# Chunk 0's units 0 and 1: the score maximum subtracted by TensorE, and the calls of one engine listed anew

## The chip, the cores and the metric

The kernel runs on one core of a Trainium2 chip. The time is the device time of one execution in microseconds (us); a kernel's time is the median of its runs. The engines go by short names: PE is TensorE (PEld its weight loads), DVE is VectorE, ACT is ScalarE, POOL is GpSimd, SP is SyncE, which issues DMA transfers. Each engine works through its own instructions in the order in which they stand; between engines semaphores make one wait for another.

## The reference

Two stages. First an attention over blocks: q, k and v are 4 batches x 8 heads x 768 positions x 64, cut into 8 blocks of 96. A matrix of 8x8 for each head, `sort_net`, is normalised five times by rows and columns and mixes the blocks of k and v. Each block of q then attends to its mixed block alone. The result, 3072 tokens x 512, goes through a layer with a cosine gate.

```python
for _ in range(5):
    P = np.exp(P - np.max(P, axis=-1, keepdims=True))
    P = P / (np.sum(P, axis=-1, keepdims=True) + 1e-09)
    P = P / (np.sum(P, axis=-2, keepdims=True) + 1e-09)
k_sorted = np.einsum('bhij,bhjcd->bhicd', P, k_b)      # v_sorted likewise
scores = scale * np.matmul(q_b, k_sb.transpose(0, 1, 2, 4, 3))
scores = scores - np.max(scores, axis=-1, keepdims=True)
attn = np.exp(scores)
attn = attn / (np.sum(attn, axis=-1, keepdims=True) + 1e-09)
x = np.matmul(attn, v_sb)                  # then heads side by side: 3072 x 512
h = x @ w_in                               # 512 -> 2048
out = (h * np.cos(h)) @ w_out              # 2048 -> 512
```

## The kernel before

The 3072 tokens are cut into 8 chunks (`n`) of 384: four units (`u`) of 96 positions, all 8 heads. For a unit PE makes 8 score tiles of 96x96 in PSUM (`s_ps`, tile `sc`), DVE takes the maximum of each row and head (`s_max`, tile `mx`) and subtracts it into SBUF (`s_sub`, tile `s`), and ACT takes the exponential (`expo`, tile `p_buf`). PE turns the probabilities (`p_ps`, tile `pps`), an engine copies them to SBUF (`p_ev`, tile `p_turned`), PE weights the values with them (`av_products`, tile `av`; a column of ones beside the values gives the sums), DVE normalises (`av_norm`, tiles `r` and `xn`), PE turns the result (`x_ps`, tile `xps`), and an engine copies it into `xT` (`x_ev`).

Chunk 0 goes ahead as soon as the mixing matrix is there, so its keys are made by `kp` (48 products in three tiles `ks`) and copied by `k_place` in halves of four units, its values by `v0` in eight groups of 8 dimensions (tile `vs`) and copied by `v0e` into `vS`. `v_permute` on POOL brings the columns of dimensions 32 to 63 into order for groups 4 to 7. The mixing matrix is spread for these products by `block` on PE and `spread` on DVE (tiles `bl`, `bd`, `bdv`).

The layer is `h` = up product, cosine on ACT (tile `c`), gate on DVE (tile `gg`), down product (tile `o`). For chunk 0 the up product is done in halves of the tokens: `up_four(h, g, part)` for token half `h` (units 0 and 1, or 2 and 3) and group `g` of four of the 16 feature tiles, then `cos_four`, `gate_four`, and `down_four(ts, q)` for 128 tokens `ts` and feature group `q`; `down_out` copies and stores. For chunks 1 to 7 it is `up`, `down` and the lists given to `moe_up` and `moe_down`, into which scores, keys and values of later chunks are put.

The order of work is that of the calls in the program, written out by hand: tiles come from pools in the order of the calls, `B` is a pool of three PSUM buffers of two banks (`big`) and `C` one of two buffers of a bank (`acc`), and each engine's instructions stand as its calls come. A tile of a pool can be written once the last reader of the tile before it in its buffer is done. `fill=` and `keep_warm` add matmuls on zeros that nothing reads. The exponential and the cosine need different tables on ACT, which a table load changes. GpSimd's queue also issues most loads; from the first `v_permute` to the loads of chunk 2 its order is: the four pieces of `v_permute`, four loads of `w_out`, the ones beside the values (`ones(0)`), six copies of keys for chunk 1 (`kxp`), zeros in `q_turned`, the second halves of k and v, zeros and picks, q of chunk 2, and four more pieces of `v_permute`.

Units 2 and 3 of chunk 0 stay on the old path in both kernels, and so do all units of chunks 1 to 7.

## Time and profile before

| what | value |
|---|---|
| median of 3 runs | 231.24 us (231.17 to 231.74) |
| the profiled execution | 231.24 us, of which the span of its instructions is 229.5 us |
| PE, DVE, ACT, POOL busy | 221.8, 170.8, 154.3, 95.9 us |
| PE matmuls of the layer, up and down of chunks 1 to 7 | 78.4 and 76.2 us |
| read from HBM, written | 27.27 MB, 6.29 MB |

A row of the timeline has the start in us, the duration in us, the engine, the line in the kernel, the operation, the tile written and the tile read with partitions x elements, and how many such instructions are put together; in brackets stands the idle time of the engine before it and what ended it. A row of a group (by line and form) has, behind the first bar, the busy us of all and the mean ns of one. A row of the chain has start, duration, engine, tile and line: the chain leads back from the last instruction to what released it, or to the instruction before it on its engine.

### The profile page before, as it was taken

Reading aid. Unit: us, or ns where it says so; the run is one execution under the profiler, and the core shown is the slowest. Engines: PE = TensorE matmul, PEld = TensorE weight load, DVE = VectorE, ACT = ScalarE, POOL = GpSimd, SP = SyncE. Lnnn points to the kernel's source line nnn. Section 1 sums busy time; section 2 is a strip of 40 time slices with the busy share of each in tenths; the row PEclk is TensorE's granted clock in tenths of the full one; section 3 lists DMA queues with packets and bytes.
Section 4 is the critical chain, followed back from the end, with each engine's and each line's share of the span. In section 5 each row is a group of like instructions: output and inputs, shape, how many; then the busy total and the mean of one; then the engine's idle time right before and its main releaser. Section 6 shows DMA issues by size and latency. Waiting matters only on the chain.

```text
span 229.5 us, 5537 instructions
## 1 busy us (share of the span) xinstructions
PE 221.8 (97%) x2268; PEld 137.8 (60%) x2268; DVE 170.8 (74%) x295; ACT 154.3 (67%) x207; POOL 95.9 (42%) x121
## 2 busy tenths in 40 slices
PE   8789999999999999999999999999999999999994
PEld 3368898567765566655665456655665566555554
DVE  6769968978798778868589977987699769646700
ACT  5659877777889758797688466736674667716521
POOL 7999999399960197944509002700000000000000
PEclk9999999999999999999999999999999999999999
DMA  5999999995999799767979839953934440351012
GB/s 64 228 195 207 202 207 224 208 223 161 121 126 194 172 135 153 133 130 145 159 136 150 125 70 156 213 92 72 180 129 81 91 160 0 69 147 46 0 46 94
DMA packets 67833, 31.21 MB, mean 136 GB/s; under 512 B 56416, under 2 KB 63200, under 8 KB 67552
## 3 DMA queue, kind: packets, MB, share of 16 engines
q0 software_dynamic: 24048, 13.64, 43.6%
q1 hardware_dynamic: 43472, 17.02, 34.7%
q8 instruction: 18, 0.29, 0.5%
q10 hardware_dynamic: 288, 0.20, 0.3%
q14 instruction: 7, 0.06, 0.1%
HBM read 27.27 MB, written 6.29 MB: 146 GB/s over the span
## 4 chain that ended last, share of the span: by engine, by line
PE 85%; DVE 7%; ACT 3%; POOL 2%; issue 2%; ACTq 0%; DVEq 0%; POOLq 0%
PE h L684 32%; PE o L709 28%; PE h L873 5%; PE o L894 5%; PE av L640 3%; PE sc L453 3%; PE ks L420 2%; DVE s L840 2%; DVE mx L836 2%; PE o L1232 2%; ACT p_buf L583 1%; PE xps L671 1%; PE sc L518 1%; PE vs L464 1%; PE qps L276 1%
## 5 line engine op out<-in xcount | busy, mean ns | idle before, releaser
L684 PE MATMUL h<-xT,w_in_t 128*128 128x384 bf16 x448 | 78.4, 326 | 0.0
L709 PE MATMUL o<-w_out_t,gg 128*128 128x512 bf16 x320 | 76.2, 379 | 0.0
L688 ACT ACTIVATE c<-h,half_pi 128x768 f32<-128x768 f32 x56 | 50.5, 902 | 25.8 <-PE h L684 24.8
L692 DVE TENSOR_TENSOR gg<-c,h 128x768 bf16<-128x768 f32 x56 | 52.6, 948 | 19.4 <-ACT c L688 19.4
L684 PEld LDWEIGHTS <-w_in_t 128*128 128x128 bf16 x448 | 42.2, 98 | 26.3 <-DVE xT L267 0.6
L709 PEld LDWEIGHTS <-gg 128*128 128x128 bf16 x320 | 28.7, 98 | 28.4
L583 ACT ACTIVATE p_buf<-s 96x768 bf16<-96x768 f32 x32 | 26.6, 843 | 5.7 <-DVE s L505 4.0
L187 POOL COPY vperm<-kv 64x768 bf16<-64x768 bf16 (+2 forms) x12 | 28.4, 2406 | 4.0 <-DMA kv<-in_v_dram 4.0
L505 DVE TENSOR_TENSOR s<-sc,mx 96x384 f32<-96x384 f32 (+1 forms) x33 | 24.3, 735 | 1.6
L503 DVE TENSOR_REDUCE mx<-sc 96x4 f32<-96x384 f32 (+1 forms) x33 | 24.0, 727 | 0.2 <-PE sc L518 0.2
L653 DVE TENSOR_TENSOR xn<-av,r 96x512 bf16<-96x512 f32 x32 | 22.0, 686 | 1.1
L138 POOL DMA_DIRECT2D kv<-in_q_dram x24 | 16.0, 681 | 0.8 <-issue 0.8
L265 ACT COPY kv<-o 128x512 f32<-128x512 f32 (+2 forms) x10 | 5.2, 524 | 14.0 <-PE o L709 11.4
L265 ACT CAST kTs<-ks 128x512 bf16<-128x512 f32 (+1 forms) x18 | 11.0, 630 | 5.3 <-PE ks L420 4.4
L651 DVE RECIPROCAL r<-av 96x8 f32<-96x8 f32 x32 | 6.3, 198 | 9.4 <-PE av L640 9.0
L894 PE MATMUL o<-w_out_t,gg 128*128 128x512 bf16 x48 | 11.7, 379 | 0.0
L138 POOL DMA_DIRECT2D q_mem<-in_q_dram x16 | 10.7, 687 | 1.8 <-DMA kv<-in_v_dram 1.3
L267 DVE COPY kv<-o 128x512 f32<-128x512 f32 (+1 forms) x5 | 3.1, 612 | 11.1 <-PE o L1232 8.5
L873 PE MATMUL h<-xT,w_in_t 128*128 128x192 bf16 x128 | 11.1, 246 | 0.0
L453 PE MATMUL sc<-kTs,q_turned 128*128 128x96 bf16 x152 | 11.1, 206 | 0.0
L873 PEld LDWEIGHTS <-w_in_t 128*128 128x128 bf16 x128 | 10.5, 98 | 0.0
L611 POOL CAST held<-q_turned 96x1 f32<-96x1 bf16 x2 | 0.4, 182 | 23.8 <-DMA q_turned<-q_mem 16.2
(135 smaller groups left out, 283.4 us busy)
## 6 DMA issues: line engine op xcount, KB each, us to landing
out_dram<-kv SPq DMA_DIRECT2D x12, 256.0 KB, 2.7
out_dram<-o_s SPq DMA_DIRECT2D x10, 256.0 KB, 3.5
w_in_t<-in_moe_w_in_dram POOLq DMA_DIRECT2D x4, 512.0 KB, 11.6
w_out_t<-in_moe_w_out_dram POOLq DMA_DIRECT2D x4, 512.0 KB, 12.1
kv<-in_k_dram POOLq DMA_DIRECT2D x2, 768.0 KB, 9.9
kv<-in_v_dram POOLq DMA_DIRECT2D x2, 768.0 KB, 13.1
pair<-in_k_dram POOLq DMA_DIRECT2D x2, 768.0 KB, 12.3
kv<-in_v_dram POOLq DMA_DIRECT2D x6, 256.0 KB, 5.2
```

Source lines behind the costliest of these rows:

```text
L138: nc.gpsimd.dma_start(out=q_heads[:, i, :, e], in_=src[:, ih * IC + i, :, e])
L187: nc.gpsimd.tensor_copy(dst, src)
L503: nc.vector.reduce_max(mx[:], scv, axis=AX.X)
L505: nc.vector.tensor_tensor(s, scv, mx.to_broadcast(list(s.shape)), op=ALU.subtract)
L583: nc.scalar.activation(p[:, :, :blk], s_t.pop((n, u)).rearrange("p e h c -> p (e h) c"), AF.Exp, scale=scale)
L653: nc.vector.tensor_tensor(xn.rearrange("p h e d -> p e h d"), avv[:, :, :, :D], r.to_broadcast([blk, 2, H2, D]), op=ALU.mult)
L684: nc.tensor.matmul(h[:, f2, :w], w_in_t[:, kk, f * 128:(f + 1) * 128], xT[n][:, kk], start=(kk == 0), stop=(kk == KC - 1))
L688: nc.scalar.activation(c[:], h[:, :, :w], AF.Sin, bias=half_pi[:, 0:1])
L692: nc.vector.tensor_tensor(gt[n, fp // 2][:, f:f + 2], c[:], h[:, :, :w], op=ALU.mult)
L709: nc.tensor.matmul(o[:], gt[n, f // 4][:, f % 4, ts * 128:(ts + 1) * 128], w_out_t[:, f, :], start=(f == 0), stop=(f == FC - 1))
L873: nc.tensor.matmul(o[:, part, f2 * w:(f2 + 1) * w], w_in_t[:, kk, f * 128:(f + 1) * 128], xT[0][:, kk, h * w:(h + 1) * w], start=(kk == 0) ...
L894: nc.tensor.matmul(out_ps[ts][:], gt[0, q][:, f % 4, ts * 128:(ts + 1) * 128], w_out_t[:, f, :], start=(f == 0), stop=(f == FC - 1))
```

## The change

Units 0 and 1 of chunk 0 (`PULL`) lose `s_sub`. In its place DVE negates the maximum into two bf16 numbers, the rounded value and what the rounding left (`s_neg`, 96x8 each), and PE adds both to the scores in PSUM by products with the identity (`s_add`: two banks, two numbers, 384 columns each, accumulating). The exponential reads the scores from PSUM (`s_t` is None for these units). The score products of these units write 48 columns each and start the accumulation once a bank.

The ones beside chunk 0's values are written by ACT in the second softmax round, as the exponential of zeros, no longer by POOL.

The calls from the first key product on are listed anew, one engine's work to a call: `up`, `down`, `batch`, `k_sort_g`, `v_sort_b`, `moe_up`, `moe_down` and their like are replaced by calls for products, copies, cosine and gate apart (`uh`, `uc`, `ug`, `dn`, `dc`, `bt`, `kg`, `kge`, `vb`, `vbe` ...). The queues of GpSimd and SP keep their order, but for the ones. From the weighted values of chunk 1's unit 3 on, the order of each other engine's work is that of before too, but for the places where a call stood after five of eight matmuls of a `down` and now stands after four. What is ahead of it is another order. The diff, with the list up to that point:

```diff
@@ -366,6 +366,10 @@
             n = (D - 12 - VN) // 2 * blk
             t = vperm[64:, VN * blk + (it - 1) * n:VN * blk + it * n].bitcast(FP32)
             A.copy(t, nones[64:].to_broadcast([64, n // 2]))
+        if it == 1:
+            A.activation(
+                vS[0][:, :, D:D + 1], nones[:blk].unsqueeze(1).to_broadcast([blk, 4 * NB, 1]),
+                AF.Exp)
         normalize(it, (less if it < 4 else sorted_by)[:])
         if it < 2:
             nc.vector.memset(pick[:, nb - 1:, it * PB + PB - 1:(it + 1) * PB], 0.0)
@@ -576,13 +580,15 @@
         qk_part(n, u, [hp], pool or acc, tag)
 
     def expo(n, u, on_pe=False):
-        p = p_bufs[cnt[0] % NP]
+        p, s = p_bufs[cnt[0] % NP], s_t.pop((n, u))
         cnt[0] += 1
 
 
         nc.scalar.activation(
-            p[:, :, :blk], s_t.pop((n, u)).rearrange("p e h c -> p (e h) c"), AF.Exp,
-            scale=scale)
+            p[:, :, :blk] if s is not None else p[:, :, :blk].rearrange(
+                "p a (t x) -> p a t x", x=2),
+            s.rearrange("p e h c -> p (e h) c") if s is not None else s_view(n, u).rearrange(
+                "p a x t -> p a t x"), AF.Exp, scale=scale)
         if u == 0 and n in (NQ, NQ + 1):
 
             w = 2 * H2 * blk
@@ -632,8 +638,7 @@
             xT[n] = xtp.tile([128, KC, TC], BF16, name="xT", tag="xT")
         a = big.tile([128, 2, 512], FP32, name="av", tag="big")
         keep_warm(fill, a[:, 0], 256)
-        pT.pop((n, u))
-        pt = pT_wide.pop((n, u))
+        pt = pT_wide[n, u]
         for hp in range(2):
             for h2 in range(H2):
                 e = hp * H2 + h2
@@ -811,11 +816,12 @@
                 hp, c = a // H2, (u * H2 + a % H2) * blk
                 for x in range(2):
                     rows = slice(x * D, (x + 1) * D)
-                    m, w = a % H2 * nb + u, HT if a % H2 == H2 - 1 else 64
+                    m, w = a % H2 * nb + u, HT if u in PULL or a % H2 == H2 - 1 else 64
                     keys = kT[0][rows, 2 * hp].rearrange("p m t -> p (m t)")
                     nc.tensor.matmul(
                         o[:, x, a * HT:a * HT + w], q_of(0, hp)[rows, c:c + 128],
-                        keys[:, m * HT:m * HT + w], start=True, stop=True)
+                        keys[:, m * HT:m * HT + w], start=a == 0 or u not in PULL,
+                        stop=u not in PULL, skip_group_check=u in PULL)
             return
         if u < 2:
             by_half(n, u, o)
@@ -841,6 +847,27 @@
             s_t[n, u].rearrange("p e h (t x) -> p (e h) x t", x=2), s_view(n, u),
             ps.pop(("mx", n, u))[:].unsqueeze(2).to_broadcast([blk, 2 * H2, 2, HT]),
             op=ALU.subtract)
+
+    PULL = (0, 1, )
+
+    def s_neg(n, u):
+        mx = ps.pop(("mx", n, u))
+        t = sp.tile([blk, 2, H2, blk], FP32, name="s", tag="s")
+        less_m = ps["mn", n, u] = t[:, 0, 0, :2 * H2].bitcast(BF16).rearrange(
+            "p (z a) -> p z a", z=2)
+        nc.vector.tensor_scalar(less_m[:, 0], mx[:], -1.0, None, op0=ALU.mult)
+        nc.vector.scalar_tensor_tensor(
+            less_m[:, 1], mx[:], -1.0, less_m[:, 0], op0=ALU.mult, op1=ALU.subtract)
+
+    def s_add(n, u):
+        o, less_m = ps["s", n, u], ps.pop(("mn", n, u))
+        for x in range(2):
+            for z in range(2):
+                nc.tensor.matmul(
+                    o[:, x, :2 * H2 * HT], ident[:blk],
+                    less_m[:, z].unsqueeze(2).to_broadcast([blk, 2 * H2, HT]),
+                    start=False, stop=z == 1, skip_group_check=True)
+        s_t[n, u] = None
 
     def p_ps(n, u, pool, tag, fill=0):
         p = pb.pop((n, u))
@@ -904,190 +931,303 @@
         copy_on(eng, o_s[:], out_ps[ts][:])
         store(0, ts, o_s)
 
-    wz = iter(range(40, D, 4))
-    kz = iter(range(6, 12))
-
-    def k_next():
-        k_sort_g(next(kz) * 4, A, *C)
-
-    def w_next(eng=A, pool=None, tag="acc"):
-        v_sort_g(next(wz), 4, eng, pool or acc, tag)
-
...
+    def uh(n, fp):
+        h = ps["h", n, fp] = big.tile([128, 2, 512], FP32, name="h", tag="big")
+        for f2 in range(2):
+            f = fp * 2 + f2
+            for kk in range(KC):
+                nc.tensor.matmul(
+                    h[:, f2, :TC], w_in_t[:, kk, f * 128:(f + 1) * 128], xT[n][:, kk],
+                    start=(kk == 0), stop=(kk == KC - 1))
+
+    def uc(n, fp):
+        c = ps["c", n, fp] = cosp.tile([128, 2, TC], FP32, name="c", tag="c")
+        nc.scalar.activation(c[:], ps["h", n, fp][:, :, :TC], AF.Sin, bias=half_pi[:, 0:1])
+
+    def ug(n, fp):
+        if (n, fp // 2) not in gt:
+            gt[n, fp // 2] = gp.tile([128, 4, TC], BF16, name="gg", tag="gg")
+        f = fp % 2 * 2
+        nc.vector.tensor_tensor(
+            gt[n, fp // 2][:, f:f + 2], ps.pop(("c", n, fp))[:],
+            ps.pop(("h", n, fp))[:, :, :TC], op=ALU.mult)
...
+    blocks.append(block([pick[:, :, z * PB:(z + 1) * PB] for z in (1, 0)]))
+    kp(2, *B)
+    k_place(2, A, 1)
+    kp(0, *B)
+    values_matrix()
+    kp(1, *B)
+    k_place(0, A, 0)
+    k_place(2, A, 0)
+    v0(3, *C)
+    k_place(0, A, 1)
+    k_place(1, V, 0)
+    k_place(1, A, 1)
+    v_permute(slice(0, 64), 32, False, 8, 40)
+    v0e(3, A)
+    s_ps(0, 0)
+    s_max(0, 0)
+    s_neg(0, 0)
+    v_permute(slice(0, 64), 40, False, 8, 48)
+    v_permute(slice(0, 64), 48, False, 8, 56)
+    s_ps(0, 3)
+    v0(1, *C)
+    v0(0, *B)
+    v0e(1, A)
+    v0e(0, A)
+    s_add(0, 0)
+    expo(0, 0, True)
+    s_max(0, 3)
+    s_sub(0, 3)
+    expo(0, 3, True)
+    v_permute(slice(0, 64), 56, False, 8, 64)
+    s_ps(0, 1)
+    v0(6, *C)
+    s_max(0, 1)
+    v0(4, *C)
+    v0e(6, A)
+    s_neg(0, 1)
+    p_ps(0, 0, *B)
+    p_ev(0, 0, V)
+    s_ps(0, 2)
+    s_add(0, 1)
+    v0e(4, A)
+    v0(5, *C)
+    expo(0, 1, True)
+    s_max(0, 2)
+    v0(7, *C)
+    v0e(7, V)
+    v0e(5, A)
+    v0(2, *B)
+    p_ps(0, 1, *B)
+    p_ps(0, 3, *C, fill=1)
+    s_sub(0, 2)
+    v0e(2, A)
+    load_w_out(0)
+    p_ev(0, 1, V)
+    av_products(0, 0)
+    av_norm(0, 0, True)
+    expo(0, 2, True)
+    av_products(0, 1)
+    p_ps(0, 2, *C, fill=1)
+    p_ev(0, 3, A)
+    av_norm(0, 1, True)
+    av_products(0, 3, fill=3)
+    x_ps(0, 0, *C)
+    p_ev(0, 2, A)
+    av_products(0, 2, fill=2)
+    x_ev(0, 0, A)
+    x_ps(0, 1, *B)
+    av_norm(0, 3, True)
+    x_ps(0, 3, *C)
+    x_ev(0, 1, A)
+    q_products(1, 1, 0, 16, *B)
+    av_norm(0, 2, True)
+    x_ev(0, 3, A)
+    load_w_out(1)
+    q_place_half(1, 1, 0, V)
+    q_place_half(1, 1, 1, A)
+    q_products(1, 0, 0, 16, *C)
+    load_w_out(2)
+    load_w_out(3)
+    q_place_half(1, 0, 1, V)
+    q_place_half(1, 0, 0, V)
+    x_ps(0, 2, *C)
+    x_ev(0, 2, V)
+    up_four(0, 1, 0)
+    up_four(0, 1, 1)
+    cos_four(0, 1)
+    gate_four(0, 1)
+    up_four(0, 0, 0)
+    up_four(0, 0, 1)
+    up_four(1, 0, 0)
+    up_four(1, 0, 1)
+    cos_four(0, 0)
+    gate_four(0, 0)
+    cos_four(1, 0)
+    gate_four(1, 0)
+    kxp(2)
+    up_four(0, 3, 0)
+    up_four(0, 3, 1)
+    cos_four(0, 3)
+    gate_four(0, 3)
+    kxp(0)
+    up_four(0, 2, 0)
+    up_four(0, 2, 1)
+    kxp(1)
+    up_four(1, 2, 0)
+    cos_four(0, 2)
+    up_four(1, 2, 1)
+    cos_four(1, 2)
+    gate_four(0, 2)
+    up_four(1, 3, 0)
+    up_four(1, 3, 1)
+    z_turned(1)
+    down_four(0, 0)
+    load(kbuf, 0, kin_d[1])
+    s_ps(1, 0)
+    load(vbuf, 64, vin_d[1])
+    gate_four(1, 2)
+    cos_four(1, 3)
+    gate_four(1, 3)
+    picks(pick_pair, (2, 3))
+    s_ps(1, 1)
+    s_max(1, 0)
+    z_vperm()
+    last = block([pick_pair[:]], *C)
+    down_four(0, 1)
+    z_turned(0)
+    up_four(1, 1, 0)
+    spread(bds[1], last)
+    up_four(1, 1, 1)
+    cos_four(1, 1)
+    s_sub(1, 0)
+    p_pads()
+    s_max(1, 1)
+    s_sub(1, 1)
+    gate_four(1, 1)
+    ks(4, *C)
+    kse(4, A)
+    ks(5, *B)
+    kse(5, A)
+    down_four(0, 2)
+    down_four(0, 3)
+    s_ps(1, 3)
+    s_ps(1, 2)
+    down_four(1, 0)
+    expo(1, 0, True)
+    load_q(2)
+    down_four(1, 1)
+    expo(1, 1, True)
+    p_ps(1, 0, *B)
+    s_max(1, 3)
+    s_sub(1, 3)
+    expo(1, 3, True)
+    s_max(1, 2)
+    p_ps(1, 1, *B)
+    p_ev(1, 1, A)
+    load_pair(pair, kin_d, 0 * CD // 2, 1 * CD // 2)
+    p_ev(1, 0, V)
+    load_pair(pair, kin_d, 1 * CD // 2, 2 * CD // 2)
+    v_permute(slice(64, 128), 0, True, 16, 16)
+    down_four(1, 2)
+    av_products(1, 0)
+    v_permute(slice(64, 128), 16, True, 16, 32)
+    v_permute(slice(64, 128), 32, True, 16, 48)
+    s_sub(1, 2)
+    v_permute(slice(64, 128), 48, True, 16, 64)
+    av_products(1, 1)
+    av_norm(1, 1, True)
+    down_out(0, A)
+    av_norm(1, 0, True)
+    down_four(1, 3)
+    expo(1, 2, True)
+    p_ps(1, 3, *B)
+    x_ps(1, 1, *C)
+    p_ev(1, 3, V)
+    p_ps(1, 2, *B)
+    down_out(1, A)
+    down_four(2, 0)
+    x_ev(1, 1, A)
+    down_four(2, 1)
+    av_products(1, 3)
...
```

`uh`, `uc` and `ug` are the three parts of `up`; `dn` is four matmuls of `down`, and the others are cut from their old functions in the same way.

Three places of the order, before and now. First DVE, in chunk 0's softmax, from the first maximum to the copy of turned probabilities after the last subtraction. Names: `mx` maxima, `sc` a unit's scores, `s` the subtracted scores (or, now, the negated maximum), `p_turned` probabilities turned, `vS` values. Before:

```order
L836 TENSOR_REDUCE mx_420<-sc_391 96x8
L840 TENSOR_TENSOR s_432<-sc_391,mx_420 96x8x2x48
L836 TENSOR_REDUCE mx_461<-sc_434 96x8
L840 TENSOR_TENSOR s_513<-sc_434,mx_461 96x8x2x48
L836 TENSOR_REDUCE mx_525<-sc_465 96x8
L840 TENSOR_TENSOR s_539<-sc_465,mx_525 96x8x2x48
L836 TENSOR_REDUCE mx_554<-sc_496 96x8
L267 COPY p_turned0_136<-pps_542 96x768
L840 TENSOR_TENSOR s_580<-sc_496,mx_554 96x8x2x48
L267 COPY p_turned2_138<-pps_584 96x768
```

Now:

```order
L842 TENSOR_REDUCE mx_416<-sc_399 96x8
L858 TENSOR_SCALAR s_418<-mx_416 96x8
L859 SCALAR_TENSOR_TENSOR s_418<-mx_416,s_418 96x8
L842 TENSOR_REDUCE mx_465<-sc_423 96x8
L846 TENSOR_TENSOR s_467<-sc_423,mx_465 96x8x2x48
L842 TENSOR_REDUCE mx_497<-sc_471 96x8
L858 TENSOR_SCALAR s_509<-mx_497 96x8
L859 SCALAR_TENSOR_TENSOR s_509<-mx_497,s_509 96x8
L267 COPY p_turned0_136<-pps_512 96x768
L842 TENSOR_REDUCE mx_554<-sc_522 96x8
L267 CAST vS_106<-vs_556 96x64x8
L846 TENSOR_TENSOR s_595<-sc_522,mx_554 96x8x2x48
```

The units come in the order 0, 3, 1, 2 in both. Two subtractions of 96x768 are gone, two pairs on 96x8 are there, the first copy of turned probabilities stands one maximum earlier, and a copy of values stands ahead of the last subtraction.

Second ACT, from the copies of chunk 0's last turned probabilities to its first cosines (`c` from `h`); `xps` are turned results, `qps` the turned q of chunk 1. Before:

```order
L265 COPY p_turned1_137<-pps_594 96x768
L265 COPY p_turned3_139<-pps_635 96x768
L265 COPY xT_607<-xps_648 128x4x96
L265 COPY xT_607<-xps_678 128x4x96
L265 COPY q_turned1_92<-qps_693 64x2x4x96
L879 ACT_TABLE_LOAD
L879 ACTIVATE c_762<-h_721,half_pi_111 128x768
L879 ACTIVATE c_776<-h_741,half_pi_111 128x768
```

Now:

```order
L265 COPY p_turned1_137<-pps_585 96x768
L265 COPY p_turned3_139<-pps_624 96x768
L265 COPY xT_600<-xps_651 128x4x96
L265 COPY xT_600<-xps_669 128x4x96
L265 COPY xT_600<-xps_678 128x4x96
L265 COPY q_turned1_92<-qps_684 64x2x4x96
L906 ACT_TABLE_LOAD
L906 ACTIVATE c_753<-h_736,half_pi_111 128x768
L906 ACTIVATE c_791<-h_757,half_pi_111 128x768
```

One more copy into `xT` stands ahead of the table load, and the copy of q is of the other four heads; it waits for DVE's copy out of the same tile `qps`.

Third DVE, where chunk 1's scores start, around the spread of the second mixing matrix (`bd1`). Before:

```order
L405 TENSOR_TENSOR bd1_149<-maskp_147,bl_897 128x128
L836 TENSOR_REDUCE mx_947<-sc_926 96x8
L885 TENSOR_TENSOR gg_778<-c_936,h_907 128x4x192
L840 TENSOR_TENSOR s_970<-sc_926,mx_947 96x8x2x48
L836 TENSOR_REDUCE mx_977<-sc_938 96x8
L840 TENSOR_TENSOR s_998<-sc_938,mx_977 96x8x2x48
L836 TENSOR_REDUCE mx_1005<-sc_989 96x8
L836 TENSOR_REDUCE mx_1033<-sc_1017 96x8
L840 TENSOR_TENSOR s_1045<-sc_989,mx_1005 96x8x2x48
L840 TENSOR_TENSOR s_1056<-sc_1017,mx_1033 96x8x2x48
L651 RECIPROCAL r_1091<-av_1072 96x8
L653 TENSOR_TENSOR xn_1093<-av_1072,r_1091 96x2x4x64
```

Now:

```order
L912 TENSOR_TENSOR gg_819<-c_903,h_865 128x4x192
L842 TENSOR_REDUCE mx_922<-sc_892 96x8
L409 TENSOR_TENSOR bd1_149<-maskp_147,bl_925 128x128
L846 TENSOR_TENSOR s_962<-sc_892,mx_922 96x8x2x48
L842 TENSOR_REDUCE mx_967<-sc_913 96x8
L846 TENSOR_TENSOR s_969<-sc_913,mx_967 96x8x2x48
L912 TENSOR_TENSOR gg_755<-c_960,h_942 128x4x192
L842 TENSOR_REDUCE mx_1039<-sc_1000 96x8
L846 TENSOR_TENSOR s_1041<-sc_1000,mx_1039 96x8x2x48
L842 TENSOR_REDUCE mx_1044<-sc_1009 96x8
L267 COPY p_turned0_136<-pps_1030 96x768
L846 TENSOR_TENSOR s_1076<-sc_1009,mx_1044 96x8x2x48
```

The units now come as 0, 1, 3, 2, each subtraction right after its maximum but for the last, the gate of the group finished last stands behind two of them, and a copy of turned probabilities stands ahead of the last subtraction.

More of the change, by code (lines that the diff above doesn't have):

```diff
@@ new lines, in vbe, with dn @@
+    def vbe(b, d0, nd, eng):
+        copy_on(
+            eng, vS[0][:, b * 2 * NB:(b + 1) * 2 * NB, d0:d0 + nd],
+            ps.pop(("vb", b, d0))[:blk].rearrange("p t n -> p n t"))
+    def dn(n, ts, q):
+        if q == 0:
+            out_ps[n, ts] = acc.tile([128, Dm], FP32, name="o", tag="acc")
+        for f in range(q * 4, q * 4 + 4):
+            nc.tensor.matmul(
+                out_ps[n, ts][:], gt[n, q][:, f % 4, ts * 128:(ts + 1) * 128], w_out_t[:, f, :],
+                start=(f == 0), stop=(f == FC - 1))
@@ new lines @@
+    dn(2, 0, 1)
+    ones(1)
+    bt(('sc', 3, 3), ('vs', 0, A))
+    qr2(3, 3)
+    be("vs", 0, A)
+    dn(2, 0, 2)
+    dn(2, 0, 3)
+    dc(2, 0, nc.sync)
+    expo(3, 3)
+    bt(('vs', 1, A), ('vs', 2, A))
+    be("vs", 1, A)
+    be("vs", 2, A)
+    dn(2, 1, 0)
+    av_products(3, 0)
+    av_norm(3, 0, False)
+    dn(2, 1, 1)
+    p_hold(3, 3)
+    load_q(5)
+    av_products(3, 1)
+    av_norm(3, 1, False)
+    dn(2, 1, 2)
+    av_products(3, 2)
+    av_norm(3, 2, True)
+    dn(2, 1, 3)
+    dc(2, 1, nc.sync)
@@ L1184 @@
+    bt(('sc', 4, 0), ('vs', 3, A), ('vs', 4, A))
+    qr2(4, 0)
+    be("vs", 3, A)
+    be("vs", 4, A)
+    dn(2, 2, 0)
+    av_products(3, 3)
+    av_norm(3, 3, True)
+    dn(2, 2, 1)
+    expo(4, 0)
+    sine_next()
+    dn(2, 2, 2)
+    xp(3, 2, 3, *B)
+    xe(3, 2, 3, V)
+    dn(2, 2, 3)
+    dc(2, 2, nc.sync)
     q_transpose_dma(5)
```

500 lines of the change are left out of this document (301 added, 199 removed).

## The prediction

> **What bounds the kernel now.** I read the page's head and its chain first, to learn which engine sets the end.
>
> ```profile
> span 229.5 us, 5537 instructions
> PEclk9999999999999999999999999999999999999999
> PE 85%; DVE 7%; ACT 3%; POOL 2%; issue 2%; ACTq 0%; DVEq 0%; POOLq 0%
> ```
>
> TensorE (PE) carries 85% of the chain that ended last, at a full clock throughout. The rest must sit in few places, so next came the busy time by stretch.
>
> ```profile
> 20.00:28.00 8.00, 7.66 (x132) 6.66 (x131) 7.71 (x15) 7.11 (x12) 7.68 (x14) 1.00 1.29 204
> 28.00:36.00 8.00, 8.00 (x102) 8.00 (x100) 5.27 (x9) 6.12 (x8) 7.81 (x10) 1.00 1.28 217
> 57.00:75.00 18.00, 18.00 (x196) 11.05 (x195) 15.39 (x22) 16.05 (x23) 9.78 (x15) 1.00 1.12 141
> ```
>
> After the stretch come the busy us of PE, PE's weight loads, DVE (VectorE), ACT (ScalarE) and POOL. From 28 us PE has no gap; in 20 to 28 it does, and DVE is busy 7.71 of 8. The chain with its times shows the border.
>
> ```profile
> 14.47 0.51 PE bl L398 x16
> ...
> 15.74 0.35 PE sc L816 x16
> ...
> 16.11 0.97 DVE mx L836
> 17.10 0.95 DVE s L840
> ...
> 23.01 0.95 DVE s L840
> 23.99 0.84 ACT p_buf L583
> ...
> 27.10 0.49 PE qps L276 x16
> 27.59 0.28 PE xps L860 x4
> 27.86 3.30 PE h L873 x40
> 31.17 0.17 PE xps L860 x4
> ...
> 37.28 0.49 PE qps L276 x16
> ...
> 55.52 0.83 PE qps L276 x32
> 56.35 1.41 PE h L684 x8
> ```
>
> From 16.1 to 24 us the chain is DVE: maximum and subtraction of four score tiles (units 0, 3, 1, 2 of chunk 0). From 27.86, where the up products `h` begin, to 56.35, where chunk 1's begin, it is PE without a break: 28.49 us of work. What follows keeps its order but for four places where one matmul changes sides with its neighbour, priced at nothing because PE's total there is the same. So the answer is one difference: when chunk 1's `h` (56.35 before) will begin.
>
> **The change part by part.** These rows price the walk; the by-form rows end in mean ns of one.
>
> ```profile
> 2.40 0.07 DVE L315 MEMSET w_out_t<- 32x8 f32 x1
> 6.66 0.26 ACT L347 ACTIVATE w_out_t<-w_out_t 32x64 f32<-32x64 f32 x1 [0.98 <-DVE pair L371]
> 12.91 1.56 PE L420 MATMUL ks<-bd,kv 128*128 128x64 bf16 x48 [0.31 <-DVE bd L405]
> 14.21 5.85 POOL L187 COPY vperm<-kv 64x768 bf16<-64x768 bf16 x4 [0.48 <-DMA kv<-in_v_dram]
> 15.51 1.07 ACT L265 CAST kTs<-ks 128x512 bf16<-128x512 f32 x2 [0.86 <-DVE kTs L267]
> 18.75 0.42 PE L797 MATMUL vs<-bdv,vperm 128*128 128x64 bf16 x8
> 19.11 0.40 PE L816 MATMUL sc<-kTs,q_turned 64*128 64x64 bf16 x16
> 19.43 0.91 PE L797 MATMUL vs<-bdv,kv 128*128 128x128 bf16 x8
> 20.18 0.60 PE L254 MATMUL vs<-warm 128*128 128x512 bf16 x2
> 22.55 0.55 DVE L267 COPY p_turned<-pps 96x768 bf16<-96x768 bf16 x1
> 24.05 0.87 PE L640 MATMUL av<-vS,p_turned 96*128 96x65 bf16 x16
> 24.50 0.20 DVE L651 RECIPROCAL r<-av 96x8 f32<-96x8 f32 x1
> 24.73 0.69 DVE L653 TENSOR_TENSOR xn<-av,r 96x512 bf16<-96x512 f32 x1
> 24.74 1.54 ACT L265 COPY p_turned<-pps 96x768 bf16<-96x768 bf16 x2
> 27.63 0.79 ACT L265 COPY q_turned<-qps 64x768 bf16<-64x768 bf16 x1 [0.46 <-PE qps L276]
> 28.44 1.28 ACT L879 ACT_TABLE_LOAD   x1
> 29.27 0.54 POOL L97 DMA_DIRECT2D kv<-in_k_dram  x1
> 56.28 1.47 PE L684 MATMUL h<-xT,w_in_t 128*128 128x384 bf16 x8
> L879 ACT ACTIVATE c<-h,half_pi 128x768 f32<-128x768 f32 x8 | 7.1, 902 | 2.7 <-PE h L873 2.7
> L267 DVE CAST kTs<-ks 128x512 bf16<-128x512 f32 x4 | 2.6, 686 | 1.3 <-ACT kTs L265 1.3
> kv<-in_k_dram POOLq DMA_DIRECT2D x1, 768.0 KB, 11.8
> ```
>
> Four operations are new, so they are bounded. (1) `s_neg`: two dependent DVE operations on 96x8 in place of one 0.95 us subtraction. Below, 0.07 us each (the 32x8 memset); above, 0.3 each. Nearest is the 96x8 reciprocal, 0.20, with 0.23 to the operation that needs it: I take 0.46 for the pair. [...] (2) `s_add`: four identity products of 384 columns. `h` L684 has that width, 1.47/8 = 0.18 each: 0.73 us for a unit; below, 0.33 (four at half the width, 3.30/40 each), above, 0.9 (matmuls of 512 columns). (3) The exponential out of PSUM across two banks: below 0.84 (from SBUF), above 1.7 (twice that); nearest is the cosine row, which reads PSUM in 0.90, and I take it. (4) The ones by ScalarE, 128 elements a lane: 0.26 to 0.6; it stands in the 0.98 us that ScalarE idled before 6.66, so it costs nothing; uncovered it would delay the softmax rounds one for one. The 0.74 us memset it replaces leaves GpSimd, and the loads of keys and values behind it (29.27) are issued that much earlier; I count that as nothing, since the queue is full there (DMA share above 1.2).
>
> Now the walk, in order, "u" for a unit of chunk 0. A hand-over to PE costs 0.06.
>
> PE issues both blocks (0.36+0.51 from 12.25), the 48 key products (1.56, to 14.7) and values 24 to 31 (19.43 to 20.18: 0.75, to 15.4). The fill of three matmuls is gone. ScalarE copies keys from 13.8, 1.07 for two, the third until 15.4; DVE's one key copy (0.69) ends at 15.5. Scores u0 start at **15.55** against 15.74 in the chain.
>
> DVE: maximum u0 from 0.4 later (as 15.74 to 16.11 in the chain), 16.0 to 16.95, negation until 17.4, maximum and subtraction u3 until 19.25. Meanwhile PE: scores u3 wait for ScalarE's fourth copy, 15.9 to 16.25; values 8 to 15 and 0 to 7 until 17.7; `s_add` u0 until 18.4; scores u1 at 18.45, when the copy frees their buffer. ScalarE: exponential u0 18.55 to 19.4, u3 until 20.15.
>
> DVE: maximum u1 19.2 to 20.15, negation until 20.6, copy of u0's turned probabilities until 21.1, maximum u2 until 21.95. PE waits 0.4 for the negation, then `s_add` u1 20.7 to 21.4, values 40 to 47 and 56 to 63 (0.35 each) until 22.1; GpSimd has their columns ready by 20.06. DVE waits 0.2 for these, since it must now evacuate the last (0.69) **before** it subtracts u2: that subtraction ends at **23.75** against 23.96 in the chain. So two subtractions of 0.95 leave DVE, and two negations (0.9), a value copy (0.65) and a wait come: the DVE stretch gains only 0.2.
>
> Then exponential u2 until 24.65, ScalarE's two copies until 26.05. Weighted values of u3 start at 25.4, since u0's transposes no longer stand ahead of them; the normalising pairs (0.20+0.69) give u3 at 26.9 and u2 at 27.75. PE: transposes u3 26.95, both q products 0.49 each until 28.15, transposes u2 0.17: `h` begins at **28.3**, against 27.86: +0.44.
>
> But one q product (0.49 at 37.28) and one transpose (0.17 at 31.17) are thereby done, which were inside the dense stretch: -0.66. Of the stretch 28.49-0.66 = 27.83 is left.
>
> New waits in the stretch. DVE turns half of q only after u2 is normalised, ScalarE the other half after that (0.79, to 29.1), then the table load (1.28), cosine (0.90) and gate (0.95): the first buffer of `h` is free at 32.35, and PE needs it after 48 matmuls, at 28.3+48x0.0825 = 32.25: 0.1. Behind the last products of group 3, DVE runs gates, maxima and subtractions of chunk 1 with hardly a gap, and three PE steps meet it at the same moment: keys 5 (buffer of unit 0's scores), the weighted values of unit 0 (its turned probabilities are now copied by DVE), the transposes of unit 1. I price each at 0.1; together 0.4, between 0 and 1. Keys 4 need the second half of k, landed at 29.27+11.8 = 41.07; PE gets there at 41.5: no wait, 0.4 to spare.
>
> Sum: +0.44 - 0.66 + 0.40 = **+0.18**. The profiled execution took 231.24 us, span and 1.74 around it, and that is the median too. Forecast 231.24+0.18 = **231.4**.
>
> **The rivals.** *DVE really is relieved (faster).* If negations cost 0.07 each, the second `s_add` starts at 20.2, and everything behind it is 0.5 earlier; with the four waits gone as well, -0.22-0.5 = -0.7: 230.5. For it: DVE is the chain from 16.1 to 24. Against it: the 0.20 reciprocal, and that each identity product holds PE and its score buffer, which the old subtraction let go. Chance 0.24.
>
> *The exponential out of PSUM is slow (slower).* Place: u0 and u1. At 1.7 us instead of 0.9, u1's ends at 23.5, PE's turning of u1 waits 0.65 (it would come at 22.85) and ScalarE's last value copies, on which the weighted values wait, end 0.9 late: 231.4+0.9 = 232.3. It decides from about 1.25 us an exponential; below that the value products behind cover it. For it: no row reads two banks alternately. Against it: the cosine's 0.90. [...] Chance 0.12.
>
> *DVE becomes the bound of chunk 1 (slower).* If its run behind group 3 starts 0.3 later than walked, or has 0.3 more in it, the three waits that meet it grow by as much and by what PE then lacks in cover, to about 1.0 in all: 231.24-0.22+1.0 = 232.0. For it: 57 to 75 shows DVE at 85% even there. Against it: only one of the three waits in a row is paid in full. Chance 0.16.
>
> *It does not do what it says*: PE's products would be work without relief, the DVE time moved to other small operations. That is most of my forecast, which has chance **0.48**.
>
> **How the numbers follow.** About 0.3% (0.7 us) is what a measurement of this kernel can tell from no change. Forecast 231.4 lies within; the first rival at the edge below, the two slow ones above. Faster 0.24, same 0.48, slower 0.28. The range takes the fast rival's edge and the dearest unknown: 230.4 to 232.3.
>
> **What would show it.** Right: the second subtraction on DVE ends near 23.75, `h` begins near 28.3, chunk 1's `h` near 56.5. Wrong: a `s_neg` pair under 0.2 us, an exponential out of PSUM over 1.2, `h` before 27.6 or after 29, PE gaps behind 39 us above 1 us in sum, or a granted clock under full between 12 and 28 us.

## The result, and the profile after

| | before | after |
|---|---|---|
| median | 231.36 us (4 runs) | 232.67 us (232.60 to 232.80, 4 runs) |
| ratio after to before | | 1.0055, 95% interval 1.0043 to 1.0068 |
| profiled execution, its span | 231.24, 229.5 us | 232.8, 230.6 us |
| chunk 0's `h` begins, chunk 1's `h` begins | 27.86, 56.35 us | 29.06, 57.30 us |

The change costs 1.3 us, and the time lies above the range that was given. The granted clock is full as before, but for the last of the 40 slices:

```profile
span 230.6 us, 5530 instructions
PEclk9999999999999999999999999999999999999998
```

The chain of work that ended last, in order of time (start, duration, engine, tile, line), over the same stretch as before:

```profile
15.82 0.96 DVE mx L842
...
16.81 0.51 DVE s L858
17.32 0.02 issue
17.34 1.38 DVE s L859
18.72 0.88 DVE mx L842
...
21.47 0.18 DVE s L858
21.65 0.02 issue
21.68 0.16 DVE s L859
...
23.77 0.87 DVE s L846
...
31.34 0.91 ACT c L906
32.25 0.02 issue
32.27 0.97 DVE gg L912
33.24 0.04 issue
33.28 5.44 PE h L900 x64
...
57.30 0.76 PE h L939 x4
```

L858 and L859 are the two negations of 96x8. Unit 1's pair takes 0.34 us, less than the 0.46 of the forecast; unit 0's takes 1.9. From there on everything is late: unit 3's maximum starts at 18.64 where the walk had 17.4, the last subtraction ends at 24.63 (walk 23.75), `h` begins at 29.06 (walk 28.3). The waits of TensorE between 12 and 62 us (engine, line, who was waited for, us in total, times, longest) name the same place first:

```profile
PE sc L866 <- DVE s L859: 0.8, 1, 0.8
...
PE sc L866 <- DVE s L858: 0.5, 1, 0.5
```

What GpSimd did meanwhile shows in its timeline, copy by copy, beside VectorE's:

```profile
15.80 1.47 POOL L187 COPY vperm<-kv 64x768 bf16<-64x768 bf16 x1
17.22 1.46 POOL L187 COPY vperm<-kv 64x768 bf16<-64x768 bf16 x1
16.81 0.49 DVE L858 TENSOR_SCALAR s<-mx 96x8 bf16<-96x8 f32 x1
17.34 1.38 DVE L859 SCALAR_TENSOR_TENSOR s<-mx,s 96x8 bf16<-96x8 f32 x1
21.47 0.17 DVE L858 TENSOR_SCALAR s<-mx 96x8 bf16<-96x8 f32 x1
21.68 0.16 DVE L859 SCALAR_TENSOR_TENSOR s<-mx,s 96x8 bf16<-96x8 f32 x1
```

The first negation ends at 17.30, as the copy that began at 15.80 ends (17.27); the second at 18.72, as the next copy ends (18.68). By 20.12 GpSimd is done with its copies, and the second pair, at 21.47, is short.

### The profile page after: what moved, and what is told of

Same layout as the page of the kernel before. It is cut to its first block, busy times and chain, and to the rows that moved or that the text cites. A ratio compares the mean times of both kernels' runs of the same rounds, so it can differ in the third digit from the quotient of the medians.

```text
span 230.6 us, 5530 instructions
## 1 busy us (share of the span) xinstructions
PE 219.9 (95%) x2251; PEld 137.7 (60%) x2273; DVE 171.9 (75%) x298; ACT 153.4 (67%) x207; POOL 95.1 (41%) x120
## 4 chain that ended last, share of the span: by engine, by line
PE 83%; DVE 10%; ACT 3%; issue 2%; DMA 1%; ACTq 0%; DVEq 0%
PE h L689 18%; PE o L714 16%; PE h L939 14%; PE o L1036 11%; PE o L921 4%; PE av L645 3%; PE h L900 3%; PE sc L457 3%; PE ks L424 2%; DVE mx L842 2%; PE o L1581 2%; PE sc L522 1%; PE pps L878 1%; PE xps L990 1%; PE vs L1023 1%
## 5 line engine op out<-in xcount | busy, mean ns | idle before, releaser
L714 PE MATMUL o<-w_out_t,gg 128*128 128x512 bf16 x169 | 39.9, 379 | 0.4
L689 PEld LDWEIGHTS <-w_in_t 128*128 128x128 bf16 x256 | 24.7, 98 | 16.2
L1036 PE MATMUL o<-w_out_t,gg 128*128 128x512 bf16 x134 | 33.7, 379 | 0.6 <-issue 0.3
L187 POOL COPY vperm<-kv 64x768 bf16<-64x768 bf16 (+2 forms) x12 | 28.3, 2400 | 3.7 <-DMA kv<-in_v_dram 3.7
L587 ACT ACTIVATE p_buf<-s 96x768 bf16<-96x768 f32 x30 | 24.7, 841 | 4.9 <-DVE s L509 4.0
L939 PEld LDWEIGHTS <-w_in_t 128*128 128x128 bf16 x192 | 17.5, 98 | 9.9 <-DVE xT L267 0.3
```

The source lines that it names most:

```text
L187: nc.gpsimd.tensor_copy(dst, src)
L587: nc.scalar.activation(p[:, :, :blk] if s is not None else p[:, :, :blk].rearrange("p a (t x) -> p a t x", x=2), s.rearrange("p e h c -> p ...
L689: nc.tensor.matmul(h[:, f2, :w], w_in_t[:, kk, f * 128:(f + 1) * 128], xT[n][:, kk], start=(kk == 0), stop=(kk == KC - 1))
L714: nc.tensor.matmul(o[:], gt[n, f // 4][:, f % 4, ts * 128:(ts + 1) * 128], w_out_t[:, f, :], start=(f == 0), stop=(f == FC - 1))
L939: nc.tensor.matmul(h[:, f2, :TC], w_in_t[:, kk, f * 128:(f + 1) * 128], xT[n][:, kk], start=(kk == 0), stop=(kk == KC - 1))
L1036: nc.tensor.matmul(out_ps[n, ts][:], gt[n, q][:, f % 4, ts * 128:(ts + 1) * 128], w_out_t[:, f, :], start=(f == 0), stop=(f == FC - 1))
```

## The experiments

Each was timed beside the kernel before, with 5 to 12 runs of its own. "Outside" is the time less the span, the median of its runs; 1.78 in the kernel before. "Chunk 1's `h`" is of the one profiled run; e7 and e9, which do the work of the kernel before in its order, have it 0.26 and 0.55 later than that kernel's own profile, so up to 0.5 there is not a difference by itself.

| run | median us | ratio to before, 95% | chunk 1's `h` | span, outside (medians) |
|---|---|---|---|---|
| changed kernel | 232.67 | 1.0043 to 1.0068 | 57.30 | 230.5, 2.17 |
| e1 maxima in PSUM | 232.24 | 1.0028 to 1.0052 | 56.47 | 230.1, 2.10 |
| e11 half pieces | 232.35 | 1.0019 to 1.0043 | 56.84 | 230.2, 2.15 |
| e4 before, with a pair | 234.38 | 1.0099 to 1.0138 | 59.69 | 232.6, 1.82 |
| e2 unit 0 subtracted | 232.00 | 1.0012 to 1.0043 | 56.46 | 230.2, 1.79 |
| e3 both subtracted | 232.24 | 1.0030 to 1.0054 | 57.05 | 230.5, 1.84 |
| e12 unit 1 subtracted | 233.19 | 1.0062 to 1.0088 | 58.51 | 231.3, 1.89 |
| e5 e1 with fewer fills | 232.49 | 1.0032 to 1.0060 | 56.64 | 230.4, 2.09 |
| e6 e1 with five of eight | 232.07 | 1.0017 to 1.0041 | 56.64 | 229.95, 2.12 |
| e7 before, more on TensorE | 231.47 | 0.9993 to 1.0011 | 56.61 | 229.6, 1.87 |
| e9 before, more on ScalarE | 231.55 | 0.9993 to 1.0013 | 56.90 | 229.6, 1.94 |
| e8 q later | 231.71 | 1.0004 to 1.0022 | 56.15 | 229.6, 2.15 |
| e10 q later, unit 1 alone | 232.09 | 1.0013 to 1.0031 | 56.47 | 230.3, 1.79 |
| e13 the same, maximum in SBUF | 231.58 | 1.0006 to 1.0034 | 57.38 | 229.85, 1.81 |
| e14 q later, no unit | 232.75 | 1.0047 to 1.0079 | 56.88 | 230.85, 1.78 |

### The pair and GpSimd's copies: e1, e4, e11

Theory A: a small VectorE operation whose sources lie in SBUF has to wait for the GpSimd copy in progress. The rivals were TensorE's identity products and the new order. In e1 the maxima of units 0 and 1 lie in unused columns of their score tile in PSUM:

```diff
-        mx = ps["mx", n, u] = small.tile([blk, 2 * H2], FP32, name="mx", tag="mx")
+        if n == 0 and u in PULL:
+            mx = ps["s", n, u][:blk, 0, 2 * H2 * HT:2 * H2 * HT + 2 * H2]
+        else:
+            mx = small.tile([blk, 2 * H2], FP32, name="mx", tag="mx")
+        ps["mx", n, u] = mx
```

> The changed kernel with one edit: the row maxima of units 0 and 1 are written into the unused columns of the score tile in PSUM, so that neither negation has two inputs in SBUF or reads SBUF alone. Theory A (the negations of unit 0, 0.49 and 1.38 us in the changed kernel, waited for GpSimd's column copies, which run from 14.4 to 20.1 us and whose ends at 17.25 and 18.7 are the ends of both negations): now the pair takes about 0.45 us together, the maximum of unit 3 starts near 17.3 instead of 18.64, the up products near 28.3 instead of 29.06, and the time falls by about 0.8 us to some 231.9. Rival B (the way over TensorE costs: identity products, the held score buffer, the exponential out of PSUM): the up products stay at 29.0, time 232.6. Rival C (the new order behind 30 us costs): 232.6 as well.

VectorE's and GpSimd's timeline of e1:

```profile
16.89 0.16 DVE L862 TENSOR_SCALAR s<-sc 96x8 bf16<-96x8 f32 x1
17.08 0.16 DVE L863 SCALAR_TENSOR_TENSOR s<-sc,s 96x8 bf16<-96x8 f32 x1
16.88 1.48 POOL L187 COPY vperm<-kv 64x768 bf16<-64x768 bf16 x1
```

The same two operations, inside a copy, take 0.16 each, and the copy is none the longer for it. Chunk 1's `h` comes 0.83 us sooner. The median falls by 0.43 only, half of what was expected; where the rest goes stands under "What e1 still lacks". e4 makes the reverse test: the kernel before, with an unused pair behind unit 0's maximum.

```diff
     s_max(0, 0)
+    extra = small.tile([blk, 2, 2 * H2], BF16, name="extra", tag="extra")
+    nc.vector.tensor_scalar(extra[:, 0], ps["mx", 0, 0][:], -1.0, None, op0=ALU.mult)
+    nc.vector.scalar_tensor_tensor(
+        extra[:, 1], ps["mx", 0, 0][:], -1.0, extra[:, 0], op0=ALU.mult, op1=ALU.subtract)
```

> The kernel before, with the same pair of small VectorE operations added behind unit 0's maximum, its result read by nothing. The cost of the pair by itself. A: the pair falls under GpSimd's column copies, each of the two ends with a piece of them, and the pair takes 1 to 1.5 us; VectorE is the chain there, so the time rises by 1.0 to 1.5 us, to 232.4 to 232.9. B and C: the pair costs what small operations cost, 0.4 us, and the time rises by at most that, to 231.7.

```profile
17.10 1.50 DVE L935 TENSOR_SCALAR extra<-mx 96x8 bf16<-96x8 f32 x1
18.63 1.36 DVE L936 SCALAR_TENSOR_TENSOR extra<-mx,extra 96x8 bf16<-96x8 f32 x1
17.08 1.49 POOL L187 COPY vperm<-kv 64x768 bf16<-64x768 bf16 x1
18.52 1.45 POOL L187 COPY vperm<-kv 64x768 bf16<-64x768 bf16 x1
```

Here the first negation comes 0.02 us behind the start of a copy and pays nearly all of it; the pair costs 2.9 us of VectorE and the kernel 2.94, about twice the 1 to 1.5 expected. It also confirms that VectorE is the path there: `h` moves by 3.36 (31.22 against 27.86). The 0.46 beyond the pair goes with the granted clock: it is 0.77 from 20 to 24 us and 0.80 from 24 to 28, where the kernel before has it full. TensorE idles 3.09 us up to 20.92; whether the one brings the other is not shown. e11 leaves the changed kernel as it is and halves GpSimd's pieces, now eight copies of 0.83; all four calls are edited like this one:

```diff
-    v_permute(slice(0, 64), 40, False, 8, 48)
+    v_permute(slice(0, 64), 40, False, 4, 48)
```

> The changed kernel with GpSimd's four copies of 1.46 us between 14.4 and 20.1 cut into eight of half the size. Theory A (VectorE's small operations with both sources in SBUF wait for the copy that GpSimd is in): each of unit 0's two negations ends with a piece of 0.73 to 0.8 us, the pair takes 0.4 to 1.3 us instead of 1.91 (1.0 in the middle), h begins at 28.2 to 28.6, chunk 1's h near 56.6 (57.30 in the changed kernel), time 232.1 to 232.3. Rival (the pair is slow by itself, or waits for something else): 1.9 again, 232.7.

```profile
16.82 0.60 DVE L858 TENSOR_SCALAR s<-mx 96x8 bf16<-96x8 f32 x1
17.46 0.73 DVE L859 SCALAR_TENSOR_TENSOR s<-mx,s 96x8 bf16<-96x8 f32 x1
16.56 0.83 POOL L187 COPY vperm<-kv 64x384 bf16<-64x384 bf16 x1
17.33 0.83 POOL L187 COPY vperm<-kv 64x384 bf16<-64x384 bf16 x1
```

The wait follows the length of the piece: 1.33 for the pair, each negation ending within 0.05 of a piece, chunk 1's `h` 0.46 sooner and the median span 0.3 shorter. The three runs bear out theory A for these operations: e1 takes the SBUF source away and keeps the identity products and the order, e4 has neither of these two, e11 shortens the copy alone. Beside a copy the longest operation of each pair took 1.50 us (e4), 1.38 (the changed kernel) and 0.73 (e11) with its sources in SBUF, and 0.16 (e1) with the maximum in PSUM. By what means the copy holds the operation up, no view shows.

### The parts of the change: e2, e3, e12

e2 puts unit 0 back to VectorE's subtraction in the changed order, e12 unit 1 in the same way, e3 both:

```diff
-    PULL = (0, 1, )
+    PULL = (1, )
...
-    s_neg(0, 0)
+    s_sub(0, 0)
...
-    s_add(0, 0)
```

> The changed kernel with unit 0 on the old way again: one subtraction of 96x768 by VectorE where the pair of negations stood, no identity products for it. A: the subtraction reads scores from PSUM and maxima from SBUF, is not held up, 0.95 us instead of 1.91 for the pair and its gap; up products near 28.3, time 231.8 to 232.0. B: half of the loss goes with one of two units, 232.0. C: 232.6.

> The changed kernel's order and calls, with units 0 and 1 both on the old way: no negations, no identity products, no exponential out of PSUM. A: unit 1's pair was cheap in the changed kernel (0.37 us, GpSimd was not copying then), so its subtraction brings 0.5 us back on VectorE: slower than with unit 0 alone taken back, 232.0 to 232.3. B: faster than that run, at 231.4 or under. C: 232.6.

> The changed kernel with unit 1 subtracted by VectorE again; unit 0 keeps the pair, its maximum in SBUF, and the identity products. Theory A: unit 0's pair meets GpSimd's copies as before the edit, 1.8 to 1.9 us, and VectorE's last subtraction of chunk 0 ends 0.5 to 0.7 later than 24.63, so chunk 1's h comes at 57.6 to 57.9 and the span is 230.8 to 231.2. On the time outside the span: if it belongs to unit 0's new path alone it is 2.1, time 233.1; if it needs both units on the new path it is 1.8, time 232.8.

e2 comes within 0.01 us of e1 at chunk 1's `h`, but both are held by q's load there (below), so for unit 0 the two ways are not told apart. e12 keeps only the pair that waits (0.68 and 1.37) and is the slowest of the three. e3 shows that the new order without any identity path takes 0.8 us more than the kernel before.

### What e1 still lacks: e5, e6, e8

In e1 chunk 1's `h` is only 0.12 behind the kernel before, its time 0.8. The first cosine of a chunk, from ScalarE's timelines, shows where the rest comes from (difference to the kernel before, us; what counts is how it grows along a row):

| run | chunk 1 (57.79) | chunk 2 (85.52) | chunk 6 (184.19) | chunk 7 (206.84) |
|---|---|---|---|---|
| changed kernel | +0.95 | +1.01 | +1.01 | +1.01 |
| e1 | +0.12 | +0.33 | +0.34 | +0.66 |
| e2 | +0.11 | +0.54 | +0.55 | +0.55 |
| e5 | +0.29 | +0.74 | +0.75 | +1.26 |
| e6 | +0.29 | +0.13 | +0.14 | +0.61 |
| e7 | +0.26 | +0.11 | +0.11 | +0.11 |
| e8 | -0.20 | -0.09 | +0.09 | +0.43 |
| e13 | +1.03 | +0.97 | +1.49 | +1.85 |

Two of the places where four matmuls now stand instead of five lie between chunks 1 and 2. At the first, TensorE reaches the weighted values of chunk 2's unit 0, whose probabilities a transposing DMA brings. TensorE's timeline of e2, and of before:

```profile
76.94 0.42 PE L645 MATMUL av<-vS,p_turned 96*128 96x65 bf16 x8 [0.19 <-DMA p_turned<-p_buf]
```

```profile
76.83 0.42 PE L640 MATMUL av<-vS,p_turned 96*128 96x65 bf16 x8
```

Before, five matmuls of 0.22 stood ahead of it, now four, and in e2 the DMA has not landed, nor in e5 (a wait of 0.21). In e1 no wait shows there. At the second place, two turnings of results (`xps`) had a matmul between them and now have none. The chain of before, and of e1:

```profile
82.96 0.17 PE xps L671 x4
83.13 0.22 PE o L709
83.35 0.18 PE xps L671 x4
```

```profile
83.08 0.19 PE xps L994 x4
83.27 0.03 issue
83.30 0.34 PE xps L994 x4
```

From the start of the first turning to the end of the second it is 0.57 before, with the matmul in it, and 0.56 in e1 without it, so the matmul's 0.22 comes on top: that is e1's 0.21, and half of what e2 and e5 lose. What holds the second turning, no view names. e6 is e1 with five of eight at all three places; the first of them is shown:

```diff
     dn(1, 1, 2)
     expo(2, 3, True)
+    dn(1, 1, 3, (0,))
     av_products(2, 0)
     av_norm(2, 0, True)
-    dn(1, 1, 3)
+    dn(1, 1, 3, (1, 2, 3))
```

> The changed kernel with the maxima in PSUM, and with the three places behind 57 us put back to five of eight matmuls ahead of the neighbour. Theory D (the order of the tail): the weighted values of chunk 2's unit 0 then come 0.22 us later and no longer meet the transposing DMA of their probabilities; the loss between chunk 1's h (+0.12 against before) and chunk 2's cosines (+0.33 in the first experiment) goes, the span is 0.2 shorter, 229.9, the time 232.0. Rival (the DMA's landing sets the place either way): span 230.1, time 232.2. Outside the span 2.1 in both, since the count stays 4580.

e5 is e1 less four fill matmuls:

```diff
-    p_ps(0, 3, *C, fill=1)
+    p_ps(0, 3, *C)
...
-    p_ps(0, 2, *C, fill=1)
+    p_ps(0, 2, *C)
...
-    av_products(0, 2, fill=2)
+    av_products(0, 2)
```

> The changed kernel with the maxima in PSUM, less four fill matmuls on zeros (the one ahead of each turning of units 3 and 2, the two ahead of unit 2's weighted values). The time outside the span was 2.09 to 2.20 us in all nine runs of the changed kernel and of the first experiment, and 1.72 to 1.94 in every run of the four others. What divides them is TensorE's instruction count: 4580 against 4572 or fewer. Theory G (the count crosses a limit): with 4572 here the time outside the span falls to 1.8, the span stays that of the first experiment (229.9 to 230.5), time 231.9. Rival (it belongs to the new path of unit 0, whatever the count): 2.1 outside, 232.2.

e5 and e6 ran on the same chip and reach chunk 1 at the same place; at chunk 2 they are 0.61 apart, and their medians 0.42 (e5 also lacks the fills). So the first two places cost something, the first where TensorE is early enough to meet the DMA. The third, behind chunk 2, costs nothing: both rows grow by 0.01 up to chunk 6. Of e6's loss at chunk 7 the larger part is another wait: the `h` of the last chunk for `xT<-xn`, also a transposing DMA (0.16 in e1, 0.31 in e6, 0.18 in e8).

The second thing that holds e1 back is seen in its chain:

```profile
12.92 14.26 DMA q_mem<-in_q_dram
27.18 0.04 issue
27.22 0.57 PE qps L276 x16
...
32.41 0.04 issue
32.45 5.44 PE h L904 x64
...
56.47 1.41 PE h L943 x8
```

Chunk 1's q lands at 27.18, and the change has both its products ahead of `h`; at 0.5 each, `h` cannot begin before 28.2, however early VectorE is done. e8 (with e5's and e6's edits) puts them behind; the calls at their old places go, and unit 1's turned result now stands ahead of unit 2's weighted values:

```diff
+    up_four(0, 1, 0)
+    up_four(0, 1, 1)
     x_ps(0, 2, *C)
     x_ev(0, 2, V)
-    up_four(0, 1, 0)
-    up_four(0, 1, 1)
+    q_products(1, 1, 0, 16, *C)
     cos_four(0, 1)
...
     up_four(0, 0, 1)
+    q_products(1, 0, 0, 16, *C)
```

> Fewer fills and five of eight as in the two others, and both turnings of chunk 1's q (and unit 2's turned result) put behind the first up products of chunk 0, which need only units 0 and 1. In the first experiment both q products stood ahead of h and waited for q's load, landed at 27.2, so h began at 28.23 and the third buffer's gate held PE until 32.45. Theory C (the order of chunk 0's end is the second loss): h begins near 27.1, PE finds each buffer free, chunk 1's h comes at 56.2 (before 56.35), no loss behind it, outside 1.8: span 229.4, time 231.2, a little under before. Rival (VectorE and ScalarE have no room for q's copies between gates and cosines): a wait of 0.3 to 1 in the up products, chunk 1's h at 56.5 or later, 231.6 or more.

```profile
26.88 1.32 PE h L904 x16
28.20 0.17 PE xps L891 x4
28.37 0.49 PE qps L276 x16
28.86 1.43 PE h L904 x16
30.28 0.49 PE qps L276 x16
30.77 6.71 PE h L904 x80
...
56.15 1.41 PE h L943 x8
```

As expected up to here: no gap, and chunk 1's `h` at 56.15, the earliest of all profiles, though 0.20 ahead of the kernel before is within their scatter. The rest of the expectation failed: 0.3 goes at chunk 7, and the time outside the span stays at 2.15. The median is 231.71, 0.04 to 0.22% above before: level, no gain.

### The time outside the span: e7, e9

In all runs of the changed kernel and of e1 2.09 to 2.20 us lie outside the span, in the 78 runs of the kernel before that were timed beside the experiments 1.72 to 1.92. Instruction counts were the suspects: e7 cuts a fill of two matmuls in seven, e9 adds six one-element copies on ScalarE at 200 us, both in the kernel before.

```diff
-    v0(3, *B, fill=2)
+    v0(3, *B, fill=7, cols=146)
```

```diff
...
+        for _ in range(6):
+            nc.scalar.copy(early[:], half_pi[:])
...
```

> The kernel before, with the fill ahead of values 24 to 31 cut from two matmuls of 512 columns into seven of 146: the same work in ten more TensorE instructions, 4580 instead of 4570. Theory G: the span stays 229.3 to 229.8, the time outside it rises from 1.78 to 2.1, time 231.75. Rival (count does nothing): outside 1.78, time 231.4.

> The kernel before with six copies of one element on ScalarE behind its last early sine near 200 us, where it idles for 1.4 us; its program then has 314 instructions, waits counted. TensorE's count does not set the time outside the span: 4572 of them left it at 2.07 to 2.14 and 4580 of them in the kernel before left it at 1.81 to 1.91. What still divides the two groups is ScalarE's count: 313 in all five kernels with 2.1, 310 or 311 in the five with 1.8. Theory S (ScalarE's count crosses a limit): 2.1 outside, span 229.3 to 229.8, time 231.75. Rival (it belongs to the new path of unit 0 in another way): 1.8, time 231.4.

Both theories fall: 1.87 and 1.94, a little above 1.78 and neither at 2.1, and e5 with as few TensorE instructions as e2 stays at 2.09. What the medians divide by is whether both units are on the new path: both 2.09 to 2.17 in six kernels, unit 0 alone 1.89, unit 1 alone 1.79 to 1.81, none 1.78 to 1.94. One run of e14, with none, had 2.24. Why is open; no view shows what happens there.

### A version better than both: e10, e13, e14

e8's order with the new path for unit 1 alone (e10 with its maximum in PSUM, e13 in SBUF) and for no unit (e14), edited as in e2 and e3:

> The version with q's products behind the first up products, with the new path for unit 1 alone: unit 0 is subtracted by VectorE again, unit 1's maximum stays in PSUM. VectorE's last subtraction of chunk 0 ends some 0.2 us later (23.69 against 23.5 when unit 0 alone was put back), h begins near 27.1, chunk 1's h comes at 56.2 to 56.4 (before 56.35), ScalarE's program has 311 instructions. Theory: nothing is lost outside (1.8), span 229.3 to 229.6, time 231.2, level with the kernel before or a little under. Rival (the two identity products and the pair of unit 1 cost as much as the subtraction they replace, and the wait for the last chunk's transposing DMA, 0.2 to 0.4 in the four kernels with maxima in PSUM, comes here too): span 229.8, time 231.6.

> The version with q's products behind the first up products and the new path for unit 1 alone, now with unit 1's maximum in SBUF; its pair runs after GpSimd's copies are done, so it should take 0.33 us as in PSUM. Theory: the wait for the last chunk's transposing DMA goes with the maxima in PSUM (it was there in all five such kernels and in none of the seven others), so the loss of 0.3 near 206 us is absent: chunk 1's h at 56.3 to 56.5, span 229.5 to 229.7, outside 1.8, time 231.4, level with the kernel before. Rival (the wait is chance, or goes with the order): span 229.9 to 230.3, time 231.9.

> The same order with no unit on the new path: all four subtractions on VectorE. It tells what the identity path of unit 1 is worth beside the order. Theory: VectorE's last subtraction ends 0.6 later than with the pair, h and chunk 1's h too, 56.9 to 57.1; span 230.2, time 232.0. Rival (TensorE, without the four identity products, and ScalarE gain as much as VectorE loses): chunk 1's h at 56.5, time 231.5.

None beats the kernel before. e10 and e14 miss their forecasts upward. The profiled runs of e12 and e13, the slowest of their runs (234.21 and 233.09), had a granted clock of 0.6 to 0.7 in a slice near 20 us, and those of e3 and e4 0.8, so their positions count for little; but in e13 the wait for `xT<-xn` was there too (0.2), so that wait doesn't belong to maxima in PSUM, as e13 supposed. What it hangs on is open. The medians of e14 and e13, 232.75 and 231.58, say that unit 1's identity path is worth about 1.2 us in this order, twice the 0.6 expected; in e14's profile 0.4 and 0.2 of it are waits for transposing DMAs, near 79 and 179 us.

## Why the prediction was wrong, by its own steps

- **The bound.** Right: VectorE from 16 to 24 us, then TensorE without a gap. e4 shows the first (2.9 us on VectorE, 3.36 at `h`, 2.94 in the time).
- **(1) The pair, "below, 0.07 us each; above, 0.3 each. Nearest is the 96x8 reciprocal": the step that failed.** Measured 0.49 and 1.38 for unit 0, 0.17 and 0.16 for unit 1. The reciprocal has the shape, but it reads its source from PSUM, so its row says nothing of sources in SBUF; the pair reads SBUF, while GpSimd copies from SBUF to SBUF. The bounds took all small operations for alike and did not ask what runs beside them, though the group of the four GpSimd copies (14.21, 5.85) stood among the quoted rows. The pair took 1.9 instead of 0.46; 0.77 of that reached `h` and chunk 1's `h` (57.30 against 28.3 + 27.83 + 0.40 = 56.53). e1, which takes the wait away, gives 0.83 back at chunk 1's `h` but only 0.43 in the median, since it runs into the waits behind it.
- **(2) The identity products.** 0.84 for the four (0.73 taken). **(3) The exponential out of PSUM.** 0.81, just under the lower bound of 0.84, so the rival with a slow exponential falls; out of SBUF it took 0.84 and 0.85 before, 0.03 to 0.04 longer. ScalarE's timeline:

```profile
19.46 0.81 ACT L587 ACTIVATE p_buf<-sc 96x768 bf16<-96x768 f32 x1 [1.03 <-PE sc L866]
20.61 0.84 ACT L587 ACTIVATE p_buf<-s 96x768 bf16<-96x768 f32 x1 [0.34 <-DVE s L846]
```

- **(4) The ones on ScalarE.** 0.77 us, above the 0.26 to 0.6 of the bounds, but hidden, as said: ScalarE still idles 0.20 behind it, and the first product of chunk 0 comes at 12.26 (12.25 before).
- **Work moved out of the stretch, and its waits.** Right in sum: from `h` to chunk 1's `h` 57.30 - 29.06 = 28.24, that is 27.83 and 0.41 of waits (0.40 said). Their division was not: the third `h` buffer took 0.26 (33.28 instead of 29.06 + 48 x 0.0825 = 33.02), not 0.1.
- **`h` at 28.3.** e1, without the pair's wait, has it at 28.23 and chunk 1's `h` at 56.47, 0.06 from the forecast. In part that is luck: what holds it there is q's load, landed at 27.18, which the walk did not have.
- **The four places with one matmul less, "priced at nothing because PE's total there is the same".** Wrong in kind: a total says nothing of who is waited for. Three of the places lie behind 57 us, and two of them cost: the changed kernel, itself late, loses 0.06 up to chunk 2, e1 0.21, e2 and e5 0.43 and 0.45.
- **The time around the span** was taken as unchanged, 1.74. It grew by 0.39 in the medians (2.17 against 1.78), without a known cause.

Together: 0.18 forecast + 0.77 + 0.06 + 0.39 = 1.40; the medians differ by 1.31. So by these positions the failed step makes somewhat more than half of the miss, and the time outside the span, still open, about a third. The rival that let VectorE be relieved failed by the same step as the forecast; the sign "`h` after 29" was the one that came.
